# Second products of a third pair of token tiles by seven block products, with the end of the attention beside their first products

## The chip, the core and the metric

The kernel runs on one core of a Trainium2 chip. Its engines each have a queue of their own: TensorE (PE in the profile), VectorE (DVE), ScalarE (ACT), GpSimd (POOL) and SyncE (SP), which here only starts DMA transfers. The metric is the device time of one execution, in microseconds; lower is better. The time before is a median of 829.72 us over three runs (829.48 to 831.48).

## The reference

Linear attention over 8 batches of 8 heads, 576 rows of 64 columns each, and then a feed-forward layer on its output:

```
q_s = softmax(q) over the 64 columns;  k_s = softmax(k) over the 576 rows
kv  = k_s^T v            (64 x 64 for each batch and head)
x   = q_s kv             (gathered to 4608 tokens x 512)
out = relu(x @ w_in)^2 @ w_out      (w_in 512 x 2048, w_out 2048 x 512)
```

Inputs and output are float32.

## The kernel before

**Tiles.** `P` is 128, `M` 512, `HM` 256, `B` 8, `NF` 16, `NP` 4. The tokens are nine tiles of 512: tile `t` (0 to 7) holds the first 512 rows of batch `t`, and tile 8 holds the last 64 rows of all eight batches. For float32 accuracy every operand is split into a high and a low part (`xh`/`xl`, `gh`/`gl`, `wi_h`/`wi_l`, `wo_h`/`wo_l`, made by a ScalarE copy and a VectorE subtraction), and each product is three matmuls: high by high, high by low, low by high. All of these matmuls have a 128x128 weight and a 128x512 moving operand.

**Plain tiles.** In tiles 0 to 4 each of the 16 blocks `f` of the hidden layer takes 12 first matmuls (tile `h`), a relu and a square on ScalarE, a split into `gh` and `gl`, and 12 second matmuls into four accumulators `acc` in PSUM (`ps_o`, tags `o0` to `o3`). The second products of a block come `LA` blocks after its first ones.

**Joint tiles.** The last four tiles are taken in pairs, `JOINT` = (5, 6) and (7, 8). Of a pair, `first_products` and then `second_products` each compute a 2x2 product of blocks with seven block products and extra sums, in place of eight: 336 matmuls of the same shape for what would be 384. Between them the squared hidden layer goes through DRAM: `keep` stores its blocks `b11`, `b12`, `b21`, `b22` in `g_all`, and `load_raw` loads them back. VectorE makes the differences of the operands (`make_t`), ScalarE and VectorE split them (`split_step`). Sums of the blocks of the weights are made once, beside the plain tiles (`full_sums`, `add_sums`, `split_sums`, `rest_sums`, called a key for each pair of weight blocks; `whole_sums` is a smaller form), and stored in `w_sums` and `wo_sums`.

**Attention.** Batch 0 is done in a planned start, batch 1 beside tile 0. The other six batches are twelve cycles `n` of two pairs of heads each (`PAIRS_OF`), and a cycle is five steps `i`, one beside each block `f` of a plain tile: `turns` and `ORDER` say which. In `pairs_step`, step 0 shifts and exponentiates k of the first pair (`end_k`) and starts the q softmax (`blocks_exp`); step 1 does the second pair and sends the halves of its statistics `bst` to the other partitions by four DMAs (`blocks_swap`); step 2 ends the second k; step 3 loads for the next cycle, normalizes q (`blocks_norm`), runs `burst` on TensorE and transposes q (`blocks_turn`); step 4 starts the next k (`begin_k`: `k_max` on VectorE, then a maximum over the partitions on GpSimd, `k_reduce`). A `burst` is the output of the cycle before (`x_two`, tiles `x`) and kv of this cycle (`h_kv`), whose scaling `kv` goes from VectorE (`ks`) to ScalarE. `x` is stored to `x_raw` and loaded whole by `load_x`.

**Order.** The order of the instructions on each engine is that in which the Python code writes them (only the start and tile 0 go through a planner). DMAs are issued in order on the queue of the engine that names them, in the kernel before almost all on SP (`Y.dma_start`).

Of the kernel before, what the change touches and what calls it, by code (L numbers as in the profile page):

```python
# [336 lines left out]
def attention_ffn(  # L337
# [29 lines left out]
    P = 128  # L367
# [38 lines left out]
    JOINT = ((B - 3, B - 2), (B - 1, B))  # L406
# [155 lines left out]
    def load_q_blocks(b, p):  # L562

        t = att.tile([P, NG, Q], F32, tag=("q", "qt")[p % 2], name=f"q_{b}_{p}", bufs=1)
# [16 lines left out]
    def load_v(b, p):  # L581
# [9 lines left out]
        t = t[:, 0:C * W].rearrange("p (c w) -> p c w", c=C)  # L591
        (G if b < TB else V).memset(t[:, :, D:D + 1].only("ones"), 1.0, n=4)
        for j in range(2):
# [7 lines left out]
    def load_tail_kq(b, which, queue=Y):  # L601
# [3 lines left out]
            [P, GH, D], F32, tag=f"{which}t", name=f"{which}t_{b}", bufs=1  # L605
# [48 lines left out]
    def blocks_exp(b, p):  # L654
# [8 lines left out]
        )  # L663
        S.activation(out=t, in_=t, func=AF.Exp)

# [14 lines left out]
    def blocks_norm(b, *pairs):  # L680

        st = made.pop("bst").rearrange("p f n g -> p f (n g)")
        by = st[:, 4, :]
        both = st[:, 0:4, :].rearrange("p (k n) g -> p k n g", n=2)
        mx, sm = both[:, :, 0, :], both[:, :, 1, :]
# [4 lines left out]
        S.activation(out=mx, in_=mx, func=AF.Exp)  # L690
        V.tensor_tensor(out=sm, in0=sm, in1=mx, op=ALU.mult)
# [74 lines left out]
    def k_reduce(b, p):  # L766

        km = made.pop(("km", b, p))
        kmx = small([P, P], "kmx", f"kmx_{b}_{p}", 1)
        G.partition_all_reduce(kmx, km, channels=P, reduce_op=RED.max)  # L770
        made["kmx", b, p] = kmx
# [193 lines left out]
    def burst(n):  # L965
# [3 lines left out]
        if n:  # L969
            x_two(*PAIRS_OF[n - 1][1], x_next if PAIRS_OF[n - 1][1][0] == TB else None, shared)  # L970
# [38 lines left out]
    def x_two(b, p, x, spare=None):  # L1009
# [4 lines left out]
        if spare is None:  # L1014
            spare = made["spare_h"] = ps_h.tile([P, M], F32, tag="h", name=f"h_x_{b}_{p}")
# [14 lines left out]
        if x is None:  # L1030
            x, here_x = att.tile([P, 2, M], F32, tag="qn", name=f"x_{b}_{p}", bufs=1), slice(0, 2)
        else:
            here_x = here
# [8 lines left out]
        if (b, p // 2) in x_raw:  # L1042
            Y.dma_start(out=x_raw[b, p // 2], in_=x)
        if p == NP - 1:
            Y.dma_start(out=x_tail[:, :, b * TL:(b + 1) * TL], in_=xt, kb=128)
# [17 lines left out]
    def first_part(t, f, x, p):  # L1063
        if p == 0:
# [3 lines left out]
                else made.pop("spare_h", None) or ps_h.tile([P, M], F32, tag="h", name=f"h_{t}_{f}")  # L1068
# [1130 lines left out]
```

## Time and profile before

| what | value |
|---|---|
| median of 3 runs | 829.72 us |
| the profiled execution | 830.97 us, with a span of 829.0 us from its first to its last instruction |
| granted TensorE clock | 0.999 |
| DMA traffic | 145.48 MB, mean 175 GB/s |

Times within the profile are in us from the span's start. Tiles 1 to 4 lie between about 135 and 512 us; the four joint phases follow (first and second products of tiles 5 and 6, then of 7 and 8). A matmul's busy time is longer than its distance from the next, since matmuls overlap; the distance is what counts here. "Busy" of a group is the union of its instructions.

### The profile page before, as it was taken

The page shows a single profiled execution, that of the slowest core. Times are in us where ns is not written, and L with a number is a line of the kernel's source. Part 1 is how long each engine was busy: PE and PEld are TensorE (multiplying, and loading weights), DVE is VectorE, ACT ScalarE, POOL GpSimd, SP SyncE. Part 2 cuts the span into 40 slices and gives each one's busy share as a digit, 9 for nine tenths or more (in the row PEclk, how much of TensorE's full clock was granted, in tenths as well). Part 3 has the DMA queues.
Part 4 walks back from the last instruction along what each step waited for, and adds up shares of the span by engine and source line. Part 5 has one row for each costly group of instructions (what it writes and reads, how often), then busy time and mean ns, then how long its engine had stood idle before and what let it go on. Part 6 is the DMA issues. An engine that isn't in the chain of part 4 may idle for free.

```text
span 829.0 us, 12870 instructions
## 1 busy us (share of the span) xinstructions
PE 816.2 (98%) x4411; PEld 662.5 (80%) x4411; DVE 620.5 (75%) x1134; ACT 481.7 (58%) x882; POOL 143.9 (17%) x151
## 2 busy tenths in 40 slices
PE   8999999999999999999999999999999999999997
PEld 7677777788888888788888787888888888888886
DVE  6888876877668656878667675577888987866995
ACT  6988844665655555655565566455754545665442
POOL 5889990001001001001001000000310000000000
PEclk9999999999999999999999999999999999999999
DMA  9993114435535446355446452766776778579455
GB/s 274 379 342 129 39 28 135 124 111 147 120 115 125 128 160 173 99 170 119 117 134 148 151 141 96 235 225 212 261 283 196 226 229 238 181 237 385 136 173 98
DMA packets 219297, 145.48 MB, mean 175 GB/s; under 512 B 146528, under 2 KB 193120, under 8 KB 219232
## 3 DMA queue, kind: packets, MB, share of 16 engines
q1 hardware_dynamic: 213312, 142.96, 56.9%
q10 hardware_dynamic: 5920, 1.71, 0.9%
q8 instruction: 35, 0.57, 0.3%
q14 instruction: 30, 0.25, 0.1%
HBM read 97.52 MB, written 46.66 MB: 174 GB/s over the span
## 4 chain that ended last, share of the span: by engine, by line
PE 84%; DMA 5%; SPq 4%; DVE 4%; ACT 2%; issue 1%; POOL 0%; DVEq 0%; ACTq 0%
PE acc L100 22%; PE h L100 20%; PE out L1865 18%; PE h L1308 17%; SPq L100 4%; PE h_kv L100 2%; PE x L100 2%; DMA k<-in_k_dram 1%; DMA qn<-in_k_dram 1%; DMA raw<-in_moe_w_out_dram 1%; DMA ring<-w_sums 1%; DVE bst L100 1%; ACT r L100 1%; DVE km L100 0%; DMA kt<-in_k_dram 0%
## 5 line engine op out<-in xcount | busy, mean ns | idle before, releaser
L100 PE MATMUL h<-xh,w 128*128 128x512 f32 x632 | 208.8, 392 | 1.0 <-ACT xh L100 0.8
L100 PE MATMUL acc<-w,gh 128*128 128x512 f32 x632 | 197.2, 393 | 0.0
L1865 PE MATMUL out<-w,w 128*128 128x512 f32 x636 | 148.9, 389 | 0.0
L100 PEld LDWEIGHTS h<-xh,w 128*128 128x128 f32 x632 | 118.6, 188 | 27.9 <-ACT xh L100 1.3
L1865 PEld LDWEIGHTS out<-w,w 128*128 128x128 f32 x636 | 119.3, 188 | 25.1 <-DVE w L100 0.2
L100 PEld LDWEIGHTS acc<-w,gh 128*128 128x128 f32 x632 | 117.0, 188 | 26.3 <-issue 1.7
L100 PE MATMUL acc<-w,gl 128*128 128x512 f32 x316 | 123.1, 390 | 0.0
L100 PE MATMUL h<-xl,w 128*128 128x512 f32 x316 | 123.1, 389 | 0.0
L100 DVE TENSOR_TENSOR gl<-r,gh 128x512 fp32r<-128x512 f32 x64 | 44.1, 688 | 73.2 <-ACT gh L100 72.6
L100 ACT ACTIVATE r<-h 128x512 f32<-128x512 f32 x79 | 47.1, 596 | 85.2 <-PE h L100 85.0
L100 POOL PARTITION_ALL_REDUCE kmx<-km x24 | 26.7, 1111 | 337.2 <-DVE km L100 337.2
L100 PEld LDWEIGHTS h<-xl,w 128*128 128x128 f32 x316 | 59.4, 188 | 12.5 <-DVE xl L100 0.4
L100 PEld LDWEIGHTS acc<-w,gl 128*128 128x128 f32 x316 | 59.3, 188 | 12.4
L1308 PE MATMUL h<-w,w 128*128 128x512 f32 x288 | 69.2, 389 | 0.0
L100 ACT COPY u<-h 128x512 f32<-128x512 f32 x48 | 28.0, 583 | 62.8 <-PE h L1308 62.7
L1308 PEld LDWEIGHTS h<-w,w 128*128 128x128 f32 x288 | 54.1, 188 | 11.2
L100 ACT CAST gh<-r 128x512 fp32r<-128x512 f32 x64 | 39.5, 617 | 21.5 <-PE acc L100 21.0
L100 ACT CAST w<-w 128x1024 fp32r<-128x1024 f32 (+1 forms) x38 | 38.0, 1006 | 18.4 <-PE out L1865 8.7
L1308 PE MATMUL h<-w,ring 128*128 128x512 f32 x192 | 46.4, 390 | 0.2 <-DMA ring<-w_sums 0.2
L100 DVE TENSOR_TENSOR c<-h,u 128x512 f32<-128x512 f32 x48 | 33.0, 687 | 13.6 <-ACT u L100 7.0
L1308 PEld LDWEIGHTS h<-w,ring 128*128 128x128 f32 x192 | 35.9, 188 | 8.1 <-PE h L1308 0.6
L100 POOL TENSOR_TENSOR w<-w,raw 128x512 int32<-128x512 int32 x32 | 41.8, 1327 | 1.7 <-DVE w L100 1.1
(236 smaller groups left out, 1290.1 us busy)
## 6 DMA issues: line engine op xcount, KB each, us to landing
w<-wo_sums SPq DMA_DIRECT2D x64, 256.0 KB, 3.4
g_b<-c SPq DMA_DIRECT2D x60, 256.0 KB, 2.6
w<-g_b SPq DMA_DIRECT2D x18, 512.0 KB, 7.8
raw<-in_moe_w_in_dram SPq DMA_DIRECT2D x16, 512.0 KB, 7.9
raw<-in_moe_w_out_dram SPq DMA_DIRECT2D x16, 512.0 KB, 8.5
v<-in_v_dram SPq DMA_DIRECT2D x56, 128.0 KB, 3.0
q<-in_q_dram SPq DMA_DIRECT2D x96, 72.0 KB, 2.3
k<-in_k_dram SPq DMA_DIRECT2D x20, 256.0 KB, 4.1
```

The source lines that it names most:

```text
L100: getattr(self.eng, op)(*map(real, args), **{k: real(a) for k, a in kwargs.items()})
L1308: nc.tensor.matmul(out=out.real(), lhsT=a[:, k * P:(k + 1) * P].real(), rhs=m[k].real(), start=(begin and k == 0 and i == 0), stop=(k == 1 ...
L1865: nc.tensor.matmul(out=banks[name][m].real(), lhsT=a[:, m * P:(m + 1) * P].real(), rhs=b[:, i, :].real(), start=fresh and j == i == k == 0 ...
```

## The change

Tiles 3 and 4 become a third pair, but only for the second products. Their first products stay plain (`first_only`): 12 matmuls for each of 16 blocks, with the relu and the square on ScalarE, and without the split into `gh` and `gl`. Each result `c` is stored in `g_all`, or straight to where the second products want it, by a DMA on GpSimd's queue, one block later (`keep_waiting`). Then `second_products(0, None)` runs for the pair. Of the other parts:

- The cycles 0 to 5 of the attention lie beside tiles 1 and 2; the six others, from `CLOSE` = 6 on, lie beside the 32 blocks of `first_only`, in a new order of steps (`close_step`). There the halves of `bst` are swapped by four ScalarE copies (`halves_swap`), `x` goes to DRAM on GpSimd's queue (`put`), and q rotates through three buffers, one of them `closing[0]`.
- `k_max` no longer reduces in one VectorE instruction for these batches; it takes the maximum of halves in two or three. v of a pair of heads comes by one DMA rather than two.
- All weight sums are made in tiles 1 and 2 (six keys in tile 1, four keys and six whole sums in tile 2; before, about three keys in each of tiles 1 to 4).
- The preparation of tiles 5 and 6 (`ahead`) is gone; `prepare_x` in the second products of tiles 3 and 4 does it, as it did for 7 and 8.
- GpSimd does no more sums or differences in the joint phases.

```
-    JOINT = ((B - 3, B - 2), (B - 1, B))
+    JOINT = ((B - 5, B - 4), (B - 3, B - 2), (B - 1, B))
...
+        if b > CLOSE // 2 + 1 and p % 2:
+            km, other = (small([P, P], "dg", f"km{i}_{b}_{p}") for i in range(2))
+            for i, to in enumerate((km, other)):
+                V.tensor_tensor(
+                    out=to.rearrange("p (h d) -> p h d", h=2), in0=kr[:, :, 2 * i, :],
+                    in1=kr[:, :, 2 * i + 1, :], op=ALU.max,
+                )
+            V.tensor_tensor(out=km, in0=km, in1=other, op=ALU.max)
...
+            V.tensor_tensor(out=halves, in0=kr[:, :, 0:2, :], in1=kr[:, :, 2:4, :], op=ALU.max)
+            V.tensor_tensor(out=km, in0=km, in1=both[:, P:2 * P], op=ALU.max)
...
+    def halves_swap():
+        st = made["bst"]
+        for j in range(2):
+            for a in range(2):
+                at, of = j * D + a * Q, j * D + (1 - a) * Q
+                S.copy(out=st[at:at + Q, 2:4, :, :], in_=st[of:of + Q, 0:2, :, :])
...
+    def close_step(n, i):
+        if i == 0:
+            if front:
+                blocks_turn(*front[0])
+                if one:
+                    load_q_blocks(*two)
+                blocks_turn(*front[1])
+            if one:
+                end_k(*one)
+                if front:
+                    end_k(*two)
...
+        elif i == 1:
+            if "put" in made:
+                made.pop("put")()
+            if later:
...
+                for p in later[:1 if front is None else 2]:
+                    load_kq(*p, "k")
+                load_q_blocks(*later[0])
+        elif i == 2:
...
+            blocks_shift(*one)
+            blocks_power(*one)
+            blocks_sum(*one)
+        elif i == 3:
+            blocks_shift(*two)
+            blocks_power(*two)
+        else:
+            blocks_sum(*two)
+            halves_swap()
+            if later:
+                begin_k(*later[0])
+            blocks_weigh()
+            if later:
+                begin_k(*later[1])
+            blocks_norm(one[0], one[1], two[1])
+            burst(n)
...
+                for p in later:
+                    load_v(*p)
...
+    SUMS_AT = {
+        1: [(KEYS[i], (f, f, f + 1)) for i, f in enumerate((2, 4, 7, 9, 12, 14))],
+        2: [(KEYS[6 + i], (f, f, f + 1)) for i, f in enumerate((2, 4, 7, 9))],
+    }
+    WHOLE_AT = {2: [(2, 11), (3, 12), (4, 13), (5, 14), (6, 14), (7, 0)]}
...
+    def first_only(i, s, f, x):
+        t = JOINT[0][i]
+        h = ps_o.tile([P, M], F32, tag=f"o{(i * NF + s) % (C - 1)}", name=f"h_{t}_{f}")
+        for p, (xh, xl) in enumerate(x):
+            for k, (w, m) in enumerate(((wi_h, xh), (wi_h, xl), (wi_l, xh))):
+                T.matmul(
+                    out=h, lhsT=w[f][:, p * P:(p + 1) * P], rhs=m,
+                    start=p == k == 0, stop=(p == NP - 1 and k == 2),
+                )
+        if i and f == NF - 4:
+            return h, temp("v", f"raw_b11_0_{f}", att, 2)
+        c = ffn.tile([P, M], F32, tag=("r", "gh")[s % 2], name=f"c_{t}_{f}")
+        return h, c
...
+    for i, t in enumerate(JOINT[0]):
...
+        for s in range(NF):
+            f = s if i == 0 or s < NF - 4 else (NF - 2, NF - 1, NF - 4, NF - 3)[s - NF + 4]
+            todo = [turns[t, s]] if turns[t, s] else []
+            if i == 0 and s >= NF - 2:
+                todo = [turns[t, s - 1], turns[t, s]] if s == NF - 1 else []
+            h, c = first_only(i, s, f, x)
+            if i == 0 and s == NF - 5:
+                split_next(later_x, t + 1, 0)
+            elif i == 0 and s == NF - 1:
+                split_next(later_x, t + 1, 1, 2, 3)
+            S.activation(out=c, in_=h, func=AF.Relu)
+            if i or f % 2:
+                S.activation(out=c, in_=c, func=AF.Square)
+            if waiting:
+                keep_waiting()
+            waiting.append((i, f, c))
+            for one in todo:
+                close_step(*one)
+            if i == 0 and s == 7:
+                x_next = load_x(t + 1)
+            if i:
+                raw_first(s)
...
     for k in range(len(JOINT)):
         now["k"] = k
-        raw.clear()
-        second_products(k, first_products(k))
+        if k:
+            raw.clear()
+        second_products(k, first_products(k) if k else None)
```

Three places show how the order of the instructions moves. In the names, `_4_3` is tile 4, block 3; `_6_2` is batch 6, head pair 2.

ScalarE, tile 4, around the end of the cycle of batch 6, pairs 2 and 3, before:

```order
L100 ACTIVATE r_4_3_4707<-h_4_3_4694 128x512
L100 ACTIVATE r_4_3_4707<-r_4_3_4707 128x512
L100 ACTIVATE bst_6_2_4525<-bst_6_2_4525 128x2x36
L100 COPY xt_6_4743<-h_kv_6_3_4728 128x128
L100 COPY x_6_1_4745<-x_6_1_0_4733 128x2x256
L100 COPY x_6_1_4745<-x_6_1_1_4736 64x2x256 x2
L100 ACTIVATE kv0_93<-h_kv_6_3_4728,ks_6_2_4770 64x64 x2
L100 ACTIVATE kv1_95<-h_kv_6_3_4728,ks_6_3_4773 64x64 x2
L100 CAST gh_4_3_4783<-r_4_3_4707 128x512
L100 ACTIVATE r_4_4_4830<-h_4_4_4817 128x512
```

And there in the change:

```order
L100 ACTIVATE q_6_3_4349<-q_6_3_4349 128x576
L100 ACTIVATE c_4_2_4434<-h_4_2_4421 128x512
L100 ACTIVATE c_4_2_4434<-c_4_2_4434 128x512
L100 COPY bst_6_2_4396<-bst_6_2_4396 32x72 x4
L100 ACTIVATE bst_6_2_4396<-bst_6_2_4396 128x2x36
L100 COPY xt_6_4479<-tails_9_4464 128x128
L100 COPY closing_1_3845<-x_6_1_0_4469 128x2x256
L100 COPY closing_1_3845<-x_6_1_1_4472 64x2x256 x2
L100 ACTIVATE kv0_93<-h_kv_6_3_4484,ks_6_2_4505 64x64 x2
L100 ACTIVATE kv1_95<-h_kv_6_3_4484,ks_6_3_4508 64x64 x2
L100 ACTIVATE c_4_3_4536<-h_4_3_4523 128x512
```

The four copies are new, the cast of `gh` is gone, and the relu of the next block stands behind the whole end of the cycle, as before, but a block is now 12 matmuls and not 24.

TensorE, from tile 3 to tile 4, before:

```order
L100 MATMUL acc_3_3_3736<-w15_1580,gh_3_14_4496 128x512 x2
L100 MATMUL acc_3_3_3736<-w15_1580,gl_3_14_4498 128x512
L100 MATMUL acc_3_3_3736<-w15_1580,gh_3_15_4541 128x512 x2
L100 MATMUL acc_3_3_3736<-w15_1580,gl_3_15_4543 128x512
L100 MATMUL h_4_0_4595<-xh_4_0_4545,w0_543 128x512
```

And in the change:

```order
L100 MATMUL h_3_15_4318<-xh_3_3_3671,w14_1559 128x512
L100 MATMUL h_3_15_4318<-xl_3_3_3673,w14_1559 128x512
L100 MATMUL h_3_15_4318<-xh_3_3_3671,w14_1559 128x512
L100 MATMUL h_4_0_4379<-xh_4_0_4171,w0_559 128x512
L100 MATMUL h_4_0_4379<-xl_4_0_4173,w0_559 128x512
```

The 24 second matmuls that ended a tile, with the split of the next `x` ahead of them, no longer stand between the two.

GpSimd, in the last cycles, in the change (before, its queue held only the two maxima of each cycle here, and no DMA):

```order
L100 DMA x_raw_6_1_155<-closing_1_3845 128x1024
L100 DMA x_tail_99<-xt_6_4479 512x1x64
L100 DMA w1_684<-c_4_9_4782 128x512
L100 DMA w7_1074<-c_4_10_4802 128x512
L100 DMA w1_684<-c_4_11_4826 128x512
```

Every block's result and every `x` is now a DMA on this queue.

More of the change, by code (lines that the diff above doesn't have):

```diff
@@ L1041, in x_two, with put @@
             S.copy(out=x[at, here_x, HM:M], in_=other[of])
[L1042 to L1045, printed above, removed]
+        queue = Y if here_x is here or not closed else G
+        def put():
+            if (b, p // 2) in x_raw:
+                queue.dma_start(out=x_raw[b, p // 2], in_=x)
+            if p == NP - 1:
+                queue.dma_start(out=x_tail[:, :, b * TL:(b + 1) * TL], in_=xt, kb=128)
+        if queue is Y:
+            put()
+        else:
+            made["put"] = put
     def x_tiles(t):
@@ L1184, in rest_sums @@
             at = slice(i * M, (i + 1) * M)
-            sums_by(key).tensor_tensor(out=lo[:, at], in0=sums[:, at], in1=hi[:, at], op=ALU.subtract)
+            V.tensor_tensor(out=lo[:, at], in0=sums[:, at], in1=hi[:, at], op=ALU.subtract)
     def keep_sums(key):
@@ L1556, in sums_step @@
             for work, when in zip((full_sums, all_sums, rest_sums), at):
-                if f == when and f:
+                if f == when:
                     work(key)
+            if f == at[2]:
+                keep_sums(key)
     def all_sums(key):
@@ L1690, in attention_ffn, with keep @@
                 x_next = load_x(t + 1)
-            if t == WT - 1:
-                ahead(f, x_next)
         if t == 0:
             plan.run(SEEDS, fill)
-        if t < WT - 1:
-            x = split_x(x_next, t + 1)
-            end_tile(t, parts, acc, NF - 2, NF - 1)
-            if t == 0:
-                load_q(TB, 1)
-                load_v(TB, 1)
-                begin_k(TB, 0)
-    units = [(t, f, parts[f], acc, c, 0, NF - 1) for f in (NF - 2, NF - 1) for c in range(C)]
-    def unit(count):
-        for t, f, parts_u, acc_u, c, begin, end in units[:count]:
-            second(f, parts_u, acc_u, c, begin=begin, end=end)
-            if f == end:
-                store(t, acc_u, c)
-        del units[:count]
-    def keep(kind, n, c):
-        Y.dma_start(out=g_all[now["k"]][kind, n // 2][:, n % 2, :], in_=c)
+        x = split_x(x_next, t + 1)
+        end_tile(t, parts, acc, NF - 2, NF - 1)
+        if t == 0:
+            load_q(TB, 1)
+            load_v(TB, 1)
+            begin_k(TB, 0)
+    def keep(kind, n, c, queue=Y):
+        queue.dma_start(out=g_all[now["k"]][kind, n // 2][:, n % 2, :], in_=c)
     def square(c, eng):
@@ new lines, in square_raw, with split_next @@
+    def square_raw(kind, j):
+        for one in raw[kind, j]:
+            S.activation(out=one, in_=one, func=AF.Square)
+    def split_next(x, t, *ps):
+        for p in ps:
+            hi, lo = (
+                ffn.tile([P, M], F32R, tag="gl" if p == 0 else f"x{c}{p}", name=f"x{c}_{t}_{p}",
+                         bufs=None if p == 0 else 1)
+                for c in "hl"
+            )
+            S.copy(out=hi, in_=x_next[:, p, :])
+            V.tensor_tensor(out=lo, in0=x_next[:, p, :], in1=hi, op=ALU.subtract)
+            x.append((hi, lo))
@@ new lines, in attention_ffn, with keep_waiting @@
+    KIND = (("b12", "b22"), ("b11", "b21"))
+    waiting = []
+    def keep_waiting():
+        i, f, c = waiting.pop(0)
+        kind, j = KIND[i][f % 2], f // 4
+        if i == 0 or j < 2:
+            keep(kind, f // 2, c, G)
+        elif (kind, j) == ("b11", J - 1):
+            if f // 2 % 2:
+                last = temp("v", f"raw_b11_0_{f}", att, 2)
+                G.dma_start(out=last, in_=c)
+                c = last
+            raw[kind, j] = (c,) + raw.get((kind, j), ())
+        else:
+            if (kind, j) not in raw:
+                raw[kind, j] = (raw_place("b21") if kind == "b11" else raw_slab(j),)
+            G.dma_start(out=raw[kind, j][0][:, f // 2 % 2, :], in_=c)
```

271 lines of the change are left out of this document (154 added, 117 removed), and 1 row of the table PLACES.

## The prediction

> **What bounds the kernel now.** I read the page first, then the stages, then the chain of work that ended last. The page's busy times put TensorE at nearly the whole span:
>
> ```profile
> PE 816.2 (98%) x4411; PEld 662.5 (80%) x4411; DVE 620.5 (75%) x1134; ACT 481.7 (58%) x882; POOL 143.9 (17%) x151
> ```
>
> The stages (stretch, its length, then PE, PEld, DVE, ACT and POOL busy, clock, DMA share, GB/s) are tiles 1, 2, 3, 4, the hand-over to the joint phases, and one second-product phase:
>
> ```profile
> 135.20:233.00 97.80, 97.62 (x567) 79.64 (x567) 69.96 (x143) 54.66 (x107) 7.27 (x7) 1.00 0.51 140
> 233.00:329.00 96.00, 95.74 (x579) 78.20 (x578) 66.81 (x137) 54.67 (x107) 7.64 (x6) 1.00 0.49 137
> 329.00:425.00 96.00, 95.77 (x579) 78.24 (x578) 67.08 (x137) 54.59 (x108) 6.24 (x6) 1.00 0.49 136
> 425.00:512.00 87.00, 86.50 (x555) 70.09 (x554) 59.04 (x118) 51.55 (x101) 5.52 (x5) 1.00 0.43 123
> 520.00:530.00 10.00, 9.84 (x44) 7.85 (x43) 3.80 (x7) 2.94 (x5) 0.00 (x0) 1.00 0.88 278
> 598.30:671.90 73.60, 73.60 (x326) 60.70 (x325) 67.43 (x87) 37.85 (x53) 3.50 (x2) 1.00 0.71 230
> ```
>
> TensorE is idle for 0.2 to 0.5 us in a tile and not at all in the second products, even where VectorE is busy for 92%. So the time is what TensorE issues. The chain gives its pitch and the price of a burst:
>
> ```profile
> 353.30 2.72 PE acc L100 x12
> 356.02 2.72 PE h L100 x12
> ...
> 399.63 2.04 PE acc L100 x9
> ...
> 402.05 0.87 PE x L100 x14
> 402.91 1.32 PE h_kv L100 x40
> 404.23 0.90 PE acc L100 x3
> ```
>
> Twelve matmuls take 2.72 us, 0.2267 each; a burst takes 404.23 - 401.67 = 2.56 us.
>
> **Matmuls removed.** Second products of two tiles are 2 x 16 x 12 = 384 matmuls, as block products 336. The 48 that go were on the path: 48 x 0.2267 = -10.9 us. The idle time of tiles 3 and 4 and of the hand-over goes with those stages: 0.23 + 0.50 + 0.16 = -0.9 us. The new pair's second phase and its hand-over to first products repeat phases that the stage rows show full; they cost nothing more as long as ScalarE has room for the late squares and the last `x` (eight squares of 0.6 and copies of 2.0 by the rows of the loop below, some 7 us more, on 38 of 74).
>
> **Tiles 1 and 2.** What one attention cycle costs beside a plain tile I take from one whole cycle, by all engines and then by tiles: `gl`, `km` and `full_o`, then `r` (DVE, ACT), and `sums_h_o`, the cast of a sum and the difference from it (DVE, ACT):
>
> ```profile
> 374.22:404.23 30.01, 30.01 (x186) 24.51 (x185) 20.39 (x43) 16.30 (x33) 2.91 (x2) 1.00 0.45 118
> ...
> 374.22:404.23 30.01, 7.79 (x20) 3.75 (x20) 3.45 (x5) 1.00 0.45 118
> ...
> 374.22:404.23 30.01, 0.00 (x0) 0.00 (x0) 2.74 (x4) 2.91 (x2) 1.00 0.45 118
> ...
> 374.22:404.23 30.01, 2.79 (x6) 0.00 (x0) 1.00 0.45 118
> ...
> 374.22:404.23 30.01, 3.45 (x5) 9.26 (x15) 1.00 0.45 118
> ...
> 374.22:404.23 30.01, 1.28 (x2) 1.14 (x2) 0.00 (x0) 1.00 0.45 118
> ```
>
> A key of sums costs VectorE 2.79 + 1.28 = 4.07 us. Tile 1 gets three more (+12.2) and one whole sum less (two additions, -1.4); tile 2 one key (+4.1) and five whole sums more (+7.2). The new `k_max` replaces 2.74 us a cycle by seven or eight short instructions, by these rows about 2.1, so -0.6:
>
> ```profile
> L100 DVE TENSOR_TENSOR sums_o<-full_o 128x256 f32<-128x256 f32 x14 | 5.9, 419 | 0.1
> L100 DVE TENSOR_TENSOR kt<-kt,kmx 64x128 f32<-64x128 f32 x24 | 6.8, 283 | 0.4
> L100 DVE TENSOR_TENSOR full_i<-w 128x512 f32<-128x512 f32 x16 | 10.9, 723 | 0.1
> L100 POOL PARTITION_ALL_REDUCE kmx<-km x24 | 26.7, 1111 | 337.2 <-DVE km L100 337.2
> ```
>
> VectorE rises to about 79 of 98 us and 76 of 96: below the 92% that hid wholly, but in bursts between in-order waits. I take +0.4 us (0 to 2): as much idle again as these tiles have now.
>
> **The closing stage** (32 blocks of first products with six cycles). A cycle lasts 5 x 2.72 + 2.56 = 16.2 us on TensorE. VectorE needs 20.39 - 3.45 - 4.07 - 0.6 = 12.3 us of it. ScalarE loses 3.1 us of casts of `gh` and the sum's 1.14, keeps relu and square (9.26 - 3.11 = 6.15 in tile 4, some 1.5 less in tile 3, where only odd blocks are squared) and attention's 5.9, and gains four swap copies, 1.0 (estimated at 0.25 each from `xt`'s 0.27 and `kv`'s 0.32 below): 13.1 us. Both fit, but they wait for each other in turn, so I add up the loop from one swap to the next:
>
> ```profile
> 430.13 0.59 ACT L100 ACTIVATE r<-h 128x512 f32<-128x512 f32 x1
> 430.75 0.63 ACT L100 ACTIVATE r<-r 128x512 f32<-128x512 f32 x1
> 432.98 0.31 ACT L100 ACTIVATE kt<-kt 64x128 f32<-64x128 f32 x1
> 437.54 0.27 ACT L100 COPY xt<-h_kv 128x128 f32<-128x128 f32 x1 [1.01 <-PE h_kv L100]
> 438.41 1.77 ACT L100 COPY x<-x 128x512 f32<-128x512 f32 x3 [0.60 <-PE x L100]
> 440.30 1.27 ACT L100 ACTIVATE kv<-h_kv,ks 64x64 f32<-64x64 f32 x4
> ...
> 434.94 0.47 DVE L100 TENSOR_TENSOR bst<-bst 128x36 f32<-128x36 f32 x2 [0.28 <-DMA bst<-bst]
> 436.56 0.23 DVE L100 TENSOR_TENSOR bst<-bst 128x72 f32<-128x72 f32 x1 [1.15 <-ACT bst L100]
> 437.70 1.43 DVE L100 TENSOR_TENSOR q<-q,bst 128x576 f32<-128x576 f32 x2
> ```
>
> Swap 1.0; two `bst` operations 0.47 and the second `k_max` 1.1; norm 1.14 (436.56 to 437.70), the two q 1.43, first `ks` 0.35; on ScalarE `kv` 1.27, relu and square 1.2, two k exponentials with tails 1.8 (shaped like the relu, 0.6, and the `kt` row), two more relus and squares 2.4, first q exponential 0.6, relu and square 1.2; VectorE's sum and shift of the second q end 1.0 later; second q exponential 0.65, relu and square 1.2. Sum 16.8 us in tile 4, about 15.3 in tile 3, against 16.2. TensorE has three banks for `h`, so a relu may be two blocks late, 5.4 us, before it stops. A 0.6 us excess in two and a half cycles hardly uses that up.
>
> At the start of tile 4, `h_4_0` needs three parts of `x` whose split stands behind the `kv` copies of ScalarE and behind `ks` on VectorE; the 5.4 us of second matmuls that covered it are gone. Counting from the last block before that burst: TensorE is there after 2.56 + 2 x 2.72 = 8.0 us and could be done at 10.7; by the loop's numbers the last `xl` is there at about 10.9 and `h_4_0` ends at 11.4: +0.7 us (0 to 2.5). At the start of the second products, the split of the first block (1024 wide; ScalarE, then VectorE) stands behind the last `kv` copies:
>
> ```profile
> L100 ACT CAST w<-w 128x1024 fp32r<-128x1024 f32 x34 | 35.8, 1052 | 18.4 <-PE out L1865 8.7 <-DMA w<-g_b 6.7 <-POOL w L100 1.0
> L100 DVE TENSOR_TENSOR w<-w,w 128x1024 fp32r<-128x1024 f32 x18 | 21.9, 1218 | 9.1 <-ACT w L100 9.0
> ```
>
> TensorE is there 10.7 us after the last burst's block, the low part after about 11.2 to 12: +1.0 us (0 to 2.5).
>
> **Transfers of the closing stage.** SP starts some 16 DMAs in a cycle instead of 24 and more; `x` and the results go to GpSimd. No trace shows a DMA issued by GpSimd. What the 16 DMA engines must carry:
>
> ```profile
> q1 hardware_dynamic: 9872, 3.51, 44.8%
> ...
> 396.00:397.00 1.00, 1.00 (x7) 0.81 (x6) 0.00 (x0) 0.43 (x3) 0.00 (x0) 1.00 1.09 385
> ...
> g_b<-c SPq DMA_DIRECT2D x60, 256.0 KB, 2.6
> ...
> k<-in_k_dram SPq DMA_DIRECT2D x20, 256.0 KB, 4.1
> ...
> 452.47 7.71 DMA qn<-in_k_dram
> ...
> 443.73 4.44 SPq L100 DMA_DIRECT2D q<-in_q_dram  x8
> ```
>
> The cycle above used 44.8% of 30 us, 13.4 us; without its 1.05 MB of sums (2.7 us at 385 GB/s) 10.7; with five results of 262 KB (3.4) 14.1 of 16.2 us, 87%. Loads of k start when the exponential has freed their buffer and must land some 6 us later by the loop; the median landing is 4.1 us, but behind a full queue one took 7.71. I take +1.5 us for all waits of this kind and the loop (0 to 8). [...]
>
> **Sum.** -10.9 - 0.9 + 0.4 + 0.7 + 1.0 + 1.5 = -8.2 us. Against the profiled execution's 830.97 that is 822.8; this execution lies 1.25 above the median, so 821.5 against 829.72. I predict 822.
>
> **Rivals.** (1) All of it hides: only -10.9 and -0.9 count, 818. For it speaks that today's tiles hide nearly everything; against it, that cycles are half as long.
> (2) Late loads: each k lands after 7.7 us and not 4.1; with 2 us of room five cycles lose 1.6 each, 8 us: 829.5, no change. For it speaks the 87%; against it, that a share of 0.88 at 520 to 530 us cost TensorE 0.16.
> (3) GpSimd's queue becomes the bound, and the kernel slower. A cycle puts 6.5 DMAs and two maxima of 1.1 us on it. If a DMA holds the queue for all of the 2.6 us that a store on SP takes to land, the cycle is 6.5 x 2.6 + 2.2 = 19.1 us, 2.9 too long; six cycles lose 17.7: 839. The stall begins at (16.2 - 2.2) / 6.5 = 2.15 us a DMA, and decides at 2.4. Against it: SP starts eight loads in 4.44 us, 0.56 each, and waits for none. [...]
>
> **Chances.** My forecast (819.5 to 826) 0.58, rival 1 0.12, rival 2 0.15, rival 3 0.10, something else, on the slow side, 0.05. About 0.3%, 2.5 us, is what a measurement can tell from no change. Faster: 0.58 + 0.12 + 0.04 of rival 2 = 0.74; same: 0.12; slower: 0.14. The range that leaves out no more than 0.2 is 818 to 831; the forecast's own is 819.5 to 826.
>
> **What the new profile would show.** Right: 48 matmuls fewer; PE full in the second products; between tile 2 and them, waits of PE for `xl` and `w` of 1 us or so, and few for `c`. Rival 2 would show VectorE waiting for DMAs of `k`, `qn` or `q`; rival 3 ScalarE's `c` waiting for DMA stores and VectorE's `k` for GpSimd. The forecast is wrong if a GpSimd DMA costs its queue over 2 us, or if waits between ScalarE and VectorE are longer than the rows suggest.

## The result and the profile after

The changed kernel takes 835.62 us (median of 4 runs, 834.34 to 835.90) beside 830.60 for the kernel before (4 runs, 829.48 to 831.75): a ratio of 1.0057, 95% interval 1.0037 to 1.0078. It is slower by 0.6% where 1% faster was forecast.

The page after, its span, its busy times and its chain of work that ended last:

```profile
span 834.0 us, 13026 instructions
...
PE 809.7 (97%) x4363; PEld 655.6 (79%) x4363; DVE 651.4 (78%) x1211; ACT 497.1 (60%) x908; POOL 150.9 (18%) x184
...
PE 76%; DVE 7%; DMA 7%; ACT 4%; issue 2%; SPq 2%; POOL 1%; DVEq 0%; ACTq 0%; POOLq 0%
```

The 48 matmuls are gone (4411 to 4363), and yet the span is 5.0 us longer than before's 829.0. VectorE, transfers and ScalarE have 18% of the chain. So TensorE waits, and the stretches where it does can be listed. These are all the stretches of 10 us between 230 and 820 us in which it is not busy throughout (busy time of PE with instructions, granted clock, DMA share, GB/s):

```profile
320.00:330.00 10.00, 8.81 (x40) 1.00 0.75 213
380.00:390.00 10.00, 6.80 (x23) 0.83 0.58 174
420.00:430.00 10.00, 9.38 (x53) 1.00 0.92 251
440.00:450.00 10.00, 7.21 (x23) 0.83 1.06 401
610.00:620.00 10.00, 9.23 (x41) 1.00 0.79 311
```

The timeline of TensorE names what it waited for (in brackets, idle time before the row and its releaser). The first row is the end of tile 2, the second the start of tile 4, the third a later block of tile 4, the last two the start of the second products:

```profile
329.88 0.47 PE L100 MATMUL h<-xh,w 128*128 128x512 f32 x1 [1.19 <-DVE o L100]
...
385.99 0.80 PE L100 MATMUL h<-xh,w 128*128 128x512 f32 x1 [3.20 <-ACT xh L100]
...
423.32 0.50 PE L100 MATMUL h<-xh,w 128*128 128x512 f32 x1 [0.53 <-ACT c L100]
442.97 0.50 PE L1934 MATMUL out<-w,w 128*128 128x512 f32 x1 [2.53 <-ACT raw_b L100]
443.73 7.13 PE L1934 MATMUL out<-w,w 128*128 128x512 f32 x23 [0.26 <-DVE w L100]
```

In the last row 23 matmuls take 7.13 us; at 0.2267 each (the last one shown at its full 0.39) they would take 5.4. TensorE's clock is the reason, as stretches of 1 us around the start of tile 4 show:

```profile
382.00:383.00 1.00, 0.79 (x4) 1.00 0.64 262
...
385.00:386.00 1.00, 0.01 (x1) 0.89 0.73 169
386.00:387.00 1.00, 1.00 (x2) 0.50 1.30 284
387.00:388.00 1.00, 1.00 (x3) 0.50 1.19 329
388.00:389.00 1.00, 1.00 (x3) 0.50 1.02 414
389.00:390.00 1.00, 1.00 (x5) 0.90 0.88 281
```

After a wait of 3.2 us the granted clock is 0.50 for some 3.5 us: the 8 matmuls from 385.99 to 389.56 should have taken 1.81 us, so 1.75 more are lost. The second such place loses as much. The wait of 3.2 us thus costs 5 here.

ScalarE at the start of tile 4 shows why `xh` is late:

```profile
379.62 1.78 ACT L100 COPY closing<-x 128x512 f32<-128x512 f32 x3
383.40 1.27 ACT L100 ACTIVATE kv<-h_kv,ks 64x64 f32<-64x64 f32 x4 [2.01 <-DVE ks L100]
384.70 0.60 ACT L100 ACTIVATE c<-h 128x512 f32<-128x512 f32 x1
385.32 1.66 ACT L100 CAST xh<-x 128x512 fp32r<-128x512 f32 x3
```

ScalarE is idle for 2 us for `ks`, then scales `kv`, and only then comes to the casts that TensorE has been waiting for since 382.8. Attention is late; how late, the swaps show, one in each cycle:

```profile
342.37 1.03 ACT L100 COPY bst<-bst 32x72 f32<-32x72 f32 x4
359.86 1.03 ACT L100 COPY bst<-bst 32x72 f32<-32x72 f32 x4 [0.34 <-DVE bst L100]
377.68 1.03 ACT L100 COPY bst<-bst 32x72 f32<-32x72 f32 x4
397.83 1.03 ACT L100 COPY bst<-bst 32x72 f32<-32x72 f32 x4
415.65 1.03 ACT L100 COPY bst<-bst 32x72 f32<-32x72 f32 x4
434.02 1.03 ACT L100 COPY bst<-bst 32x72 f32<-32x72 f32 x4
```

The periods are 17.5, 17.8, 20.2 (across the boundary), 17.8 and 18.4 us. The prediction gave TensorE 16.2 for a cycle; from burst to burst it takes 16.4 where it does not wait (`h_kv` at 342.23, 358.63 and 375.04 us). In the chain of these cycles stands the load of the second pair's q, behind the transpose that frees its buffer:

```profile
366.39 0.74 DVE qT L100
...
369.24 4.74 DMA closing<-in_q_dram
...
374.25 0.75 DVE bst L100
```

One more thing differs, at the very start. GpSimd makes `ident`, on which TensorE's first instructions wait. Before, and then after:

```profile
1.22 0.29 POOL masks.py:199 TENSOR_SCALAR_AFFINE_SELECT ident<-ident 128x128 f32<-128x128 f32 x1 [0.29 <-POOL ident masks.py:197]
```

```profile
8.71 0.28 POOL masks.py:199 TENSOR_SCALAR_AFFINE_SELECT ident<-ident 128x128 f32<-128x128 f32 x1 [7.78 <-DMA q<-in_q_dram]
```

The first matmul behind the last burst of tile 2 comes at 309.21 us before and at 312.19 after: 3.0 us of those 7.5 are still there, before the change's own stages begin.

### The profile page after: what moved, and what is told of

The parts are those of the page before. It is cut to its first block, busy times and chain, and to the rows that moved or that the text cites. A ratio compares the mean times of both kernels' runs of the same rounds, so it can differ in the third digit from the quotient of the medians.

```text
span 834.0 us, 13026 instructions
## 1 busy us (share of the span) xinstructions
PE 809.7 (97%) x4363; PEld 655.6 (79%) x4363; DVE 651.4 (78%) x1211; ACT 497.1 (60%) x908; POOL 150.9 (18%) x184
## 3 DMA queue, kind: packets, MB, share of 16 engines
q10 hardware_dynamic: 5920, 1.71, 0.9%
## 4 chain that ended last, share of the span: by engine, by line
PE 76%; DVE 7%; DMA 7%; ACT 4%; issue 2%; SPq 2%; POOL 1%; DVEq 0%; ACTq 0%; POOLq 0%
PE out L1934 25%; PE h L1359 18%; PE h L100 15%; PE acc L100 14%; SPq L100 2%; DVE bst L100 2%; DMA q<-in_q_dram 1%; PE x L100 1%; DMA closing<-in_q_dram 1%; PE h_kv L100 1%; ACT c L100 1%; DMA raw_b<-g_b 1%; DVE q L100 1%; DMA w<-g_b 1%; DMA kt<-in_k_dram 1%
## 5 line engine op out<-in xcount | busy, mean ns | idle before, releaser
L1934 PE MATMUL out<-w,w 128*128 128x512 f32 x942 | 224.0, 392 | 3.6 <-ACT raw_b L100 2.5
L1934 PEld LDWEIGHTS out<-w,w 128*128 128x128 f32 x942 | 177.6, 189 | 42.6 <-ACT raw_b L100 3.0
L100 PE MATMUL acc<-w,gh 128*128 128x512 f32 x376 | 117.5, 394 | 0.0
L100 PEld LDWEIGHTS acc<-w,gh 128*128 128x128 f32 x376 | 69.4, 188 | 16.0 <-issue 1.3
L100 PE MATMUL acc<-w,gl 128*128 128x512 f32 x188 | 73.4, 390 | 0.0
L100 POOL PARTITION_ALL_REDUCE km<-km x24 | 22.6, 944 | 212.8 <-DVE km L100 210.6
L100 DVE TENSOR_TENSOR w<-w,w 128x1024 fp32r<-128x1024 f32 (+1 forms) x32 | 36.7, 1153 | 24.1 <-ACT w L100 24.1
L100 ACT CAST w<-raw_b 128x512 fp32r<-128x512 f32 (+1 forms) x48 | 32.7, 693 | 30.2 <-PE out L1934 20.5
L100 ACT CAST w<-t 128x1024 fp32r<-128x1024 f32 x24 | 25.3, 1053 | 28.7 <-PE out L1934 28.7
L100 POOL TENSOR_TENSOR w<-w,w 128x512 fp32r<-128x512 f32 x32 | 41.2, 1300 | 4.6 <-ACT w L100 4.2
```

Source lines behind the costliest of these rows:

```text
L100: getattr(self.eng, op)(*map(real, args), **{k: real(a) for k, a in kwargs.items()})
L1934: nc.tensor.matmul(out=banks[name][m].real(), lhsT=a[:, m * P:(m + 1) * P].real(), rhs=b[:, i, :].real(), start=fresh and j == i == k == 0 ...
```

## The experiments

Each run was compared with the kernel before on the same chip. `ident`, the burst (the first `h_kv` of tile 1) and the span are those of the one profiled execution, in us. Of a run with one execution only the waits and periods of its profile are read: the ten executions of e5 alone spread over 7.6 us. e3, e13 and e14 leave out loads and use old tiles in their place; the other instructions are the same.

| run | median us (runs) | before | ratio, 95% interval | `ident` | burst | span |
|---|---|---|---|---|---|---|
| change | 835.62 (4) | 830.60 | 1.0057 (1.0037 to 1.0078) | 8.71 | 153.98 | 834.0 |
| e1 before, one GpSimd store | 830.11 (12) | 830.73 | 0.9995 (0.9981 to 1.0008) | 1.22 | 151.26 | 830.7 |
| e2 stores on SyncE | 832.88 (7) | 830.73 | 1.0039 (1.0024 to 1.0054) | 8.67 | 153.97 | 831.1 |
| e3 second q not loaded | 829.77 (11) | 830.73 | 0.9995 (0.9984 to 1.0005) | 8.60 | 153.90 | 827.3 |
| e4 `kv` late | 834.80 (5) | 830.73 | 1.0048 (1.0036 to 1.0060) | 8.96 | 154.11 | 830.8 |
| e5 one GpSimd operation | 831.55 (10) | 831.51 | 0.9992 (0.9966 to 1.0019) | 1.22 | 152.33 | 832.9 |
| e6 before, none behind the all-reduce | 835.04 (10) | 831.51 | 1.0047 (1.0032 to 1.0062) | 8.91 | 154.63 | 832.3 |
| e7 step ahead | 834.05 (1) | | | 9.01 | 154.26 | 832.3 |
| e8 late sum | 834.31 (1) | | | 8.65 | 153.91 | 832.5 |
| e9 v behind q | 837.34 (1) | | | 8.81 | 154.10 | 835.1 |
| e10 e8 and e9 | 834.70 (1) | | | 8.71 | 154.01 | 832.9 |
| e11 combined | 839.59 (4) | 830.92 | 1.0104 (1.0070 to 1.0138) | 1.22 | 150.49 | 837.2 |
| e12 combined, step ahead | 836.20 (1) | | | 1.22 | 153.35 | 834.4 |
| e13 no q, k, v loaded | 829.66 (1) | | | 8.79 | 154.11 | 827.9 |
| e14 no v loaded | 831.02 (1) | | | 8.77 | 154.06 | 829.2 |
| e15 e5, e2 and e4 | 831.25 (10) | 830.57 | 1.0013 (0.9995 to 1.0032) | 1.22 | 150.18 | 829.0 |
| e16 e15 and e8 | 832.64 (10) | 830.57 | 1.0017 (0.9996 to 1.0039) | 1.21 | 154.59 | 833.0 |
| e17 e15, split back | 827.08 (12) | 830.30 | 0.9963 (0.9946 to 0.9980) | 1.21 | 149.49 | 823.7 |
| e18 e17, step ahead | 825.46 (6) | 830.30 | 0.9942 (0.9922 to 0.9962) | 1.21 | 149.42 | 823.9 |

### The late start: e1, e2, then e5, e6

The first theory was that a program with GpSimd-issued DMAs starts late.

```diff
-        keep("b22", z.n, c)
+        keep("b22", z.n, c, G if now["k"] and z.n == 5 else Y)
```

> The kernel before, with a single one of its stores (a block of g, late in the last joint phase) issued by GpSimd instead of SyncE; nothing else differs. Theory (a program with any GpSimd-issued DMA holds GpSimd at its start): `ident` is made at about 8.7 us instead of 1.2, the first burst of tile 1 comes 2.7 to 3.0 us later than 151.3, and the time is 830.6 + 2.7 to 3.0 = 833.5. Rival (the late start of the changed kernel comes from something else in it, such as other loads): `ident` stays at 1.2 us and the time at 830.6.

```diff
-            keep(kind, f // 2, c, G)
+            keep(kind, f // 2, c, Y)
...
-        queue = Y if here_x is here or not closed else G
+        queue = Y
```

> The changed kernel with all 42 GpSimd-issued stores issued by SyncE at the same places. Theory of the start: `ident` at 1.2 us, everything up to tile 2 earlier by 2.7 to 3.0 us, and 835.6 - 3.0 = 832.6 if the stores are as well off on SyncE. Rival (SyncE's queue is in order, so a store that waits for its block holds the loads behind it): the start is 3.0 us better, but the closing stage's period rises above 17.8 us and eats it, 834 to 839.

It fell both ways: one such DMA moved nothing (`ident` at 1.22), and without any the start stayed late (8.67). The stores on SyncE did no harm: 1.0039 against 1.0057, with intervals that overlap, and in the profile a span 2.9 us shorter with the same start.

The order of GpSimd gives another difference. Before, its program ends like this (the first row is the last all-reduce, the second an instruction without a name):

```
L100 ISA kmx_3_5225<-km_3_5222 128x128
L100 ISA
L100 TENSOR_TENSOR t4l_5498<-x_4814,t4h_5496 128x512
L100 TENSOR_TENSOR full_o_6153<-w_1580 128x512 x2
```

Such an unnamed instruction also stands ahead of `ident`'s affine_select and of the first all-reduce: at each change from one group of operations to the other. (The traces hold it too, as MODIFY_POOL_CONFIG: at about 1 us and at 124 to 129 us in all of them, and a third time, at 410 to 490 us, in the nine whose `ident` is early and in no other.) The change gives all later tensor operations to VectorE (`sums_by`, `ON_POOL`), so that the third one is gone.

```diff
                 made.pop("put")()
+                nc.gpsimd.tensor_tensor(
+                    out=pad2[:, 0:1], in0=ident[:, 0:1], in1=ident[:, 0:1], op=ALU.mult
+                )
```

> The changed kernel with one tensor_tensor of 128x1 on GpSimd added behind its last all-reduce; its result is not used. The order of GpSimd shows an unnamed instruction ahead of `ident`'s affine_select, one ahead of the first all-reduce, and in the kernel before a third one ahead of the first tensor operation behind the last all-reduce, which the changed kernel lacks and this one has again. Theory (that instruction loads the code of the group of operations that follows, takes some 7.5 us unless that code is already there, and what is there at the start is what the execution before left): `ident` at 1.2 us, tile 1 earlier by 2.6 to 3.0 us, 835.6 - 2.8 = 832.8. Rival (the late start belongs to something else in the program, its length or its loads): `ident` stays at 8.7 us and the time at 835.6.

```diff
     def sums_by(key):
-        return G if key == late_key else V
+        return V
...
-    ON_POOL = ({("t4", 1)}, {})
+    ON_POOL = ({}, {})
```

> The kernel before with its tensor operations behind the last all-reduce (the late sums of the output weights and one part of t4) on VectorE instead of GpSimd, so that the last code that GpSimd loads is the all-reduce's. Theory of the reload: `ident` at 8.7 us, tile 1 later by 2.6 to 3.0, 830.7 + 2.8 = 833.5 and up to 1.5 more for VectorE's added work. Rival: `ident` at 1.2 us, 830.7 to 832.

Both came out. `ident` in e5 and in e6:

```profile
1.22 0.29 POOL masks.py:199 TENSOR_SCALAR_AFFINE_SELECT ident<-ident 128x128 f32<-128x128 f32 x1 [0.29 <-POOL ident masks.py:197]
```

```profile
8.91 0.28 POOL masks.py:199 TENSOR_SCALAR_AFFINE_SELECT ident<-ident 128x128 f32<-128x128 f32 x1 [7.99 <-DMA q<-in_q_dram]
```

One operation of 128x1, whose result nobody reads, brings the changed kernel to 831.55, no different from before (1.0057 becomes 0.9992); taking the last tensor operations off GpSimd makes the kernel before slower by 0.47%, 3.5 us. From the burst of tile 1 to the end, e6 and the kernel before take the same 677.7 us (832.3 - 154.63, 829.0 - 151.27), so in these two profiles all of it is the start. The load of q that the rows name as releaser can't be the cause: it is issued at 0.72 us with the early start and at 0.73 with the late one. What the runs show is the condition and the price. In the trace of the change 7.72 us lie between the MODIFY_POOL_CONFIG at the start and the affine_select, in that of before 0.06; what GpSimd does in that time no trace shows. That the instruction loads code, and that the execution before can leave that code behind, is a guess of mine that the two expectations rest on.

### What sets the closing stage's period: e3, e13, e14

```diff
                 blocks_turn(*front[0])
                 if one:
-                    load_q_blocks(*two)
+                    made["q", two[0], two[1]] = old_q
```

> The changed kernel without the load of the second pair's q in cycles 7 to 11: that pair works on the tile that the first pair of the cycle before has left (its values are wrong, its instructions the same); 20 DMAs of 72 KB are left out. Theory (this load, 5 us to landing behind a freed buffer, sets the period of the closing stage): the period falls from 17.8 to 16.2 to 16.8 us, the idle of 3.2, 0.6 and 2.8 us goes down to under 2 in all with the clock dips behind it, and the time to 835.6 - 8 = 827.5 (825.5 to 829.5). Rival (ScalarE's and VectorE's own work in program order sets 17.8 us, and the load is one of several things that come late together): the period stays above 17.4 and the time above 833.

e13 and e14 let the load functions return at once for cycles 8 to 11 with the tile of cycle 7.

> The changed kernel without any load of q, k and v for cycles 8 to 11 of the closing stage (q, k, v and their tails: the tiles of cycle 7 are used again, so the values are wrong and the instructions the same); the stores of x and of the blocks and the loads of blocks stay. Theory A (the transfers set the period; whichever load is issued last is the one that is late): from 378 us on the period is 16.2 us, TensorE's own, and the waits at the boundary and ahead of the second products are under 1.5 us each, span 834 - 9 = 825. Theory B (VectorE and ScalarE in turns set it, loads only add): the period is 16.8 to 17.3 and the waits at the two places stay over 1.5 us each, span 828 to 831.

> The changed kernel without the loads of v alone for cycles 8 to 11 (512 KB in packets of 256 bytes a cycle). Theory A: the other loads land faster (q in 3 us instead of 5), period 16.5 to 17, span 828 to 830. Theory B: q lands faster and nothing else changes: period 17.4 or more, span 832 to 834.

The last four swaps of e13, without any of these loads:

```profile
376.05 1.03 ACT L100 COPY bst<-bst 32x72 f32<-32x72 f32 x4
396.19 1.03 ACT L100 COPY bst<-bst 32x72 f32<-32x72 f32 x4
412.91 1.03 ACT L100 COPY bst<-bst 32x72 f32<-32x72 f32 x4
430.19 1.03 ACT L100 COPY bst<-bst 32x72 f32<-32x72 f32 x4
```

Periods 20.1, 16.7 and 17.3. e3 (swaps at 374.59, 394.72, 411.44, 428.71) and e14 (377.59, 397.74, 414.46, 431.73) have 20.1 to 20.2, 16.7 and 17.3 as well. So taking away the second q alone, v alone, or everything gives the same period in tile 4, 0.3 to 0.9 us above TensorE's 16.4. With the loads it was 1.1 us longer (17.8, 18.4). Theory A, transfers alone, is out. That the rest is what VectorE and ScalarE need in turns is the reading that is left, and is argued: no run shortened these turns and clearly the period with them.

The loads are not the whole of the 1.1 us either. e2 leaves out no load, and with the stores on SyncE its cycles in tile 4 take 16.7 and 17.5 us as well (the third swap is at 432.31), as do later those of e17 (16.7 and 17.7) and e18 (16.7 and 17.5):

```profile
398.08 1.03 ACT L100 COPY bst<-bst 32x72 f32<-32x72 f32 x4
414.80 1.03 ACT L100 COPY bst<-bst 32x72 f32<-32x72 f32 x4
```

From 342 to 436 us the loads of q there landed after 3.1 and 3.5 us in the median in their two kinds of buffers (`closing` and `q`), in the change after 3.7 and 5.0, at the same share of the DMA engines (0.83 and 0.82). So the 1.1 us belong to the loads beside stores issued by GpSimd, and go when either is taken away; no run shows why loads land later beside such stores. The 20.1 across the boundary is there without any of these loads, and so is TensorE's wait:

```profile
384.36 0.77 PE L100 MATMUL h<-xh,w 128*128 128x512 f32 x1 [2.82 <-ACT xh L100]
```

### Other orders in the cycle: e7, e8, e9, e10

e7 calls `close_step` ahead of the relu and square of its slot, e8 writes `blocks_sum(*one)` behind `blocks_power(*two)`, e9 moves `load_v` behind `load_q_blocks(*two)`, e10 is e8 and e9.

> The changed kernel with each step of the closing stage written ahead of the relu and square of its slot's block instead of behind them, which moves ScalarE's part of the step (exp, swap, casts) ahead of work that waits for TensorE. Theory (the loop's period is above TensorE's because its hand-overs between VectorE and ScalarE each wait for a slot's block in ScalarE's order, beside the load of q): the period falls from 17.8 to about 17 and the waits at the tile boundary and ahead of the second products fall below 1.5 us each: a span of 834 - 5 = 829. Rival (the load alone sets the period): period 17.8, span 833 or more.

> The changed kernel with the sums of the first pair's q written behind the shift of the second pair's instead of ahead of it, so that VectorE doesn't wait for the first exp (0.7 us) in each cycle. Theory (a chain through VectorE and ScalarE in turns sets the period): 0.7 us less a cycle, period 17.1, span 834 - 3 = 831. Rival (the load of q, 5 us to landing, sets it, and VectorE then waits for the load instead): period 17.8, span 834 within 0.7.

> The changed kernel with the loads of v for the next cycle (two of 256 KB, issued 1.4 us ahead of the second pair's q on SyncE) moved behind that load of q. Theory (the load of q stands in the loop's chain, and v ahead of it on the queue and on the transfers delays it): the second q lands 1.5 to 2.5 us earlier in each cycle, the period falls from 17.8 to about 16.7, the waits at the boundary and ahead of the second products fall from 6.0 to under 3 us in all, span 834 - 5 = 829. Rival (VectorE and ScalarE in turns set the period): 17.4 or more, span 832.5 or more.

> The same with the sum of the first pair's q behind the shift of the second pair's as well. If load and turns are both in the chain, each alone is covered by the other and only both together shorten it: period 16.2 (TensorE's own), waits under 1.5 us in all, span 834 - 7 = 827. If the load alone: as the run with the loads of v moved. If neither: 832 or more.

None brought what its theory said. e7's periods are 17.4, 18.4, 21.2, 17.7 and 18.6, e8's 17.8, 18.5, 19.2, 18.0 and 19.3; the spans are 1.7 and 1.5 us shorter, one profile each, which decides nothing. e10 kept waits of 1.0 to 1.9 us for v and `xh`. In e9 q did land earlier (medians of 3.0 and 3.7 us in its buffers instead of 3.7 and 5.0), v later (5.9 instead of 3.8), and TensorE waited for v where it had not before:

```profile
416.60 0.69 PE L100 MATMUL h_kv<-v,ek 128*64 128x65 f32 x16 [1.06 <-DMA v<-in_v_dram]
418.88 0.69 PE L100 MATMUL h_kv<-v,ek 128*64 128x65 f32 x16 [1.47 <-DMA v<-in_v_dram]
```

In the change the 16 DMA engines are at 0.82 on average from 342 to 436 us and above 1.0 in stretches; in e9 another order of the loads made v late in place of q.

### The two boundaries: e4, and what adds up: e11, e12, e15 to e18

e4 defers `kv_scale` and `kv_split` of the bursts of cycles 8 and 11 (`rest`):

```diff
                 split_next(later_x, t + 1, 1, 2, 3)
+                made.pop("rest")()
...
+            if i and s == NF - 4:
+                split_step(0)
             for one in todo:
                 close_step(*one)
...
-                if s == NF - 3:
-                    split_step(0)
-                elif s == NF - 2:
+                if s == NF - 2:
                     split_step(1)
+                    made.pop("rest")()
```

> The changed kernel with another order at two places only: the scaling of kv behind the bursts of cycles 8 and 11 is written behind the split of x for tile 4 and behind the first two splits for the second products, and the first of these splits stands ahead of cycle 11's last step. Theory (TensorE waits there because the casts that it needs stand on ScalarE behind copies of kv that are themselves late): the waits of 3.2 and 2.8 us fall to 1.0 and 0.5 in pieces too short to halve the clock, which saves 1.7 us more at each: 835.6 - 7.5 = 828 (826 to 830). Rival (the attention loop is late as a whole, so TensorE waits at the next place that needs it, the last x or the first difference): less than 3 us of gain, 833 or more.

The wait at the start of tile 4 went from 3.20 to 0.58 us, with the clock at 1.00, but waits for `c` of about 1 us came up in tile 4, and ahead of the second products it got worse:

```profile
382.82 0.50 PE L100 MATMUL h<-xl,w 128*128 128x512 f32 x1 [0.58 <-DVE xl L100]
...
420.18 0.50 PE L100 MATMUL h<-xh,w 128*128 128x512 f32 x1 [1.08 <-ACT c L100]
438.99 1.66 PE L1940 MATMUL out<-w,w 128*128 128x512 f32 x6 [1.70 <-ACT raw_b L100]
444.10 4.37 PE L1940 MATMUL out<-w,w 128*128 128x512 f32 x18 [3.45 <-ACT c L100]
```

The rival had foreseen that. But part of it was my own: the early split stood between cycle 11's exponential and its swap, which came 20.9 us after the one before. e11 and e12 put together the GpSimd operation of e5, e9's loads of v, e8's late sum and whole sums in other slots of tile 2; e11 adds all of e4, that split too, and e12 e7's order in its place. Both leave the stores on GpSimd's queue:

> The changed kernel with what the runs so far point to, together: the tensor_tensor on GpSimd behind its last all-reduce (2.8 us at the start), the loads of v behind the second q and the late sum (up to 7 us of waits and halved clock), kv's scaling behind the splits at the two boundaries, and the full sums at the end of tile 2 spread over earlier slots (1.2 us ahead of the output tiles). 835.6 - 2.8 - 7 - 1 = 825, 0.7% under the kernel before (823 to 829). Rival (the loop stays late): 830 to 832.

> The same, with each step of the closing stage ahead of its slot's relu and square in place of kv's scaling behind the splits. If ScalarE's order is a part of the chain, the period is 16.2 and the span that of the combined version or 1 us less; if it is not, TensorE waits up to 1 us more often for relus that stand behind exp: 1 to 3 us more.

Both came out slow (e12 in a single execution): v is late in e11, TensorE waits 2.3 us between 245 and 250 us in e11, where the moved sums now stand (e12's chain there has their additions and a store of 2.77 us), and cycle 11's swap comes 25.3 us behind the one before in e11. e15 is e5, e2 and e4 without these moves of v and of the whole sums, and e16 adds e8's late sum:

> The changed kernel with its 42 GpSimd-issued stores on SyncE, the tensor_tensor on GpSimd behind the last all-reduce, and kv's scaling behind the splits. By the single runs: 832.9 (stores on SyncE) - 2.8 (start) - 3 (no halved clock at the two boundaries) = 827, 0.4% under the kernel before. Rival (as with late kv alone, the wait goes elsewhere): 829.5 to 831.

> The same with the late sum of the first pair's q. If VectorE's wait for the first exp is in the chain now that the loads are a little faster: 1 to 3 us less, 825. If the loads are the chain: the same time within 1 us.

Neither is different from the kernel before. ScalarE in cycle 11 of e15:

```profile
427.30 1.05 ACT L100 CAST w<-w 128x1024 fp32r<-128x1024 f32 x1 [1.27 <-DMA w<-g_b]
430.30 1.03 ACT L100 COPY bst<-bst 32x72 f32<-32x72 f32 x4 [1.96 <-DVE bst L100]
```

The early split waits for its block's load, and then the swap waits for VectorE, which does the split's other half first. (The landing at 432 us that the next expectation names is another block's; the split's own came by 427.30.) e17 puts the split back behind cycle 11's last step, with `rest` behind it, and e18 adds e7's order:

```diff
-            if i and s == NF - 4:
-                split_step(0)
...
+                if s == NF - 3:
+                    split_step(0)
+                    made.pop("rest")()
```

> As the combined run with the stores on SyncE, but the first split for the second products stands where the changed kernel has it, behind cycle 11's last step (ahead of it, it waited on ScalarE for a transfer that landed at 432 us and held cycle 11), and kv's scaling of cycle 11 stands right behind that split. The wait of 4.8 us ahead of the second products goes to 2 to 2.8: 831.0 - 2.5 = 828.5 (827 to 830). Rival (a later wait takes its place): 830 to 831.5.

> The same with each step of the closing stage ahead of its slot's relu and square. If ScalarE's and VectorE's turns set the period (16.7 to 17.3 us without any loads), this shortens the turns: 0.5 us a cycle, 1 to 2.5 us less than the run beside it. If not, the relus are late instead: the same or up to 1 us more.

Both are faster than the kernel before, by 0.37% (0.20 to 0.54) and 0.58% (0.38 to 0.78): 3.2 and 4.8 us. The stage's waits in e18:

```profile
380.00:390.00 10.00, 8.87 (x91) 1.00 1.02 265
390.00:400.00 10.00, 8.29 (x37) 1.00 0.58 161
410.00:420.00 10.00, 9.70 (x41) 1.00 1.08 311
430.00:440.00 10.00, 9.15 (x40) 1.00 0.92 355
```

These are 4.0 us of idle time in pieces under 2, and the clock does not drop in this stage. Whether e18 is better than e17 stays open (the intervals overlap). Both profiles also had a burst 1.8 us earlier than the kernel before, which need not be theirs, since it scatters (last section); from the burst to the end they take 674.2 and 674.5 us against 677.7, so some 3.4 us come from the later stages. No run has the repaired start and the stores on SyncE without the late `kv`, so the share of `kv` alone was not measured; e17's waits at the start of tile 4 are 0.43 and 0.58 us, where e2's is 3.77.

## Why the prediction was wrong

The sum was -8.2 us and the span went up by 5.0, a miss of 13.2. Term by term, from the change's own rows:

| term | predicted | measured |
|---|---|---|
| 48 matmuls | -10.9 | -10.9 |
| idle time of the stages that go | -0.9 | -0.9 |
| start of the program | no term | +3.0 |
| tiles 1 and 2 | +0.4 | +1.2, at the end of tile 2 |
| start of tile 4 | +0.7 | +3.2, and 1.75 by the clock |
| start of the second products | +1.0 | +2.8, and 1.75 by the clock |
| closing stage and its transfers | +1.5 | +0.5 by itself |
| second phase and hand-over | 0 | +0.8 |
| not placed | | +1.8 |

**Matmuls, tiles 1 and 2** were right: up to the last burst of tile 2 the change is 3.0 us late, all of it from the start, so that VectorE's 16.7 us of more busy time in these tiles (153.4 against 136.8) cost nothing until the end of tile 2, where TensorE waits 1.19 us for an output tile of VectorE's (`o`).

**The start** is the step that was missing. The prediction counted VectorE's gain of sums, and left out what GpSimd's loss of them does: it was its last work of that kind. e6 prices it at 3.5 us and e5 at 4.1 (5.0 when the change and e5 are each set against the kernel before on their own chip), a quarter of the miss or somewhat more.

**The closing stage** is the term that was mis-sized. "Sum 16.8 us in tile 4" was near for the turns: 16.7 and 17.3 without loads. What failed is the sentence after it, that TensorE's three banks make an excess harmless. Loads beside GpSimd's stores put 1.1 us on each cycle (the prediction had the transfers at 87% and gave late k a chance of its own; in the chain it was the second q), so a cycle in tile 4 was not 0.6 us but 1.4 to 2.0 us longer than TensorE's 16.4. Without the second q's load the whole came to 829.77 us (e3), 5.9 less than the change, with waits of 1.86 and 1.34 us at the two boundaries in place of 3.20 and 2.79: the lateness was paid there more than within the stage. And at the start of tile 4 the banks do not help, because the casts of `x` wait for TensorE's last block of tile 3 and stand on ScalarE behind `kv`. "By the loop's numbers the last `xl` is there at about 10.9" rested on a loop that is on time; the last `xh` was there 3.2 us after TensorE wanted it.

**The clock** was in no term. The waits of 3.20 and 2.53 us halved it, for 3.5 us together. Whether the predicted stalls of 0.7 and 1.0 us would have touched it is not shown: e18's of 1.71 and 1.13 us did not, e7's of 1.19 and 0.68 us, 1 us apart, did.

**The rivals.** GpSimd's queue as the bound, at 839, was near in time and wrong in mechanism: in the change a DMA holds GpSimd for 0.54 us, a quarter of the 2.15 at which that stall begins, and it waits for ScalarE, not the reverse:

```profile
393.41 0.54 POOL L100 DMA_DIRECT2D g_b<-c  x1 [4.42 <-ACT c L100]
395.14 0.54 POOL L100 DMA_DIRECT2D g_b<-c  x1 [1.19 <-ACT c L100]
```

The prediction's 87% took GpSimd's stores to fall on the same 16 DMA engines as the loads. From 342 to 436 us in the change the queue of these stores has 26.7% of those engines' time and SyncE's 54.5%, with all the others 0.82. On SyncE the stores did no harm (e2: 1.0039 against 1.0057), while q landed sooner (3.1 and 3.5 us in place of 3.7 and 5.0) and the cycles of tile 4 got 1 us shorter. Late loads, at 829.5, were part of it: 1.1 us a cycle. The range's upper end, 831, had no place for a cost ahead of the stages nor for the clock.

The term of the 48 matmuls held: with the start repaired, the stores on SyncE and `kv` out of the casts' way, the kernel gains 3.2 us (e17) or 4.8 (e18) of the 8.2 that were forecast. The 1.8 us that are not placed stay open.

## What to carry to other kernels

When work leaves an engine, ask what that engine's last work of the kind did besides its result (here 3.5 us by e6), and look at the first microseconds of the new profile before any other. When two engines hand work to and fro beside a third, compare the loop's period with the third's with the loads in, and multiply the difference by the number of cycles: slack of a few banks is used up once, and is worth nothing where the third engine's own next input stands in the same queue (3.20 us at the start of tile 4). At such a boundary the order of an engine's work counts: put what the bounding engine waits for ahead of what only the late loop needs, but not ahead of what holds the loop itself (e15 to e17, where one split and the late `kv` behind it moved and 831.25 us became 827.08).

## What the runs showed of the hardware

- The start of an execution depended on the last group of operations that the program runs on GpSimd: `ident` at 1.21 to 1.22 us in nine profiles whose program ends with a tensor operation, at 8.60 to 9.01 in the eleven whose program ends with the all-reduce's group. So it comes 7.4 to 7.8 us later, and that is paid or not by what stands at the program's end (e5, e6). With a late `ident` the burst of tile 1 comes at 153.9 to 154.6 us; with an early one anywhere from 149.4 to 154.6. Why it scatters then was not found; it may be what widens the intervals of e5, e15 and e16.
- Idle TensorE and its clock: waits of 2.53 and of 3.20 us halved the clock (0.50) for some 3.5 us, while a wait of 3.45 in e4 and one of 2.10 in e17 did not (the clock was 1.00 there). In e15 one of 3.45 did (0.83 from 440 to 450 us), and so did much shorter pairs: 1.64 and 0.22 us in e3, 1.19 and 0.68 in e7. The stretches that hold these two pairs, in e3 and then in e7 (PE busy, clock, DMA share, GB/s):

```profile
380.00:390.00 10.00, 8.14 (x28) 0.83 0.73 214
```

```profile
380.00:390.00 10.00, 8.04 (x27) 0.83 0.73 213
```

So no length of a single wait tells in these runs whether the clock drops. What decides it is not shown.
- A store of 256 KB to DRAM that GpSimd issues takes it 0.54 to 0.56 us in the change. Between 342 and 436 us such stores (21 of them) landed after 4.0 us in the median, and e2's from SyncE after 3.7.
